# Attention scores and values of 24 float32 heads moved from half-array to full-array matrix products

## Chip, cores and metric

One NeuronCore of one Trainium2 chip runs the whole program. The metric is the device time of one execution in microseconds (us), given as the median of three runs. Its engines appear below under the names of the profile: PE is TensorE (matrix products), PEld its weight loads, DVE is VectorE, ACT is ScalarE, POOL is GpSimd, and SP is SyncE, whose queue issues the transfers.

## What is computed

Windowed attention with a few always visible "sink" keys, and behind it a feed-forward layer with a cosine gate. Sizes: 4 batches, 8 heads, 768 positions, head size 64, window 128, 4 sink positions, model width 512, inner width 2048.

```python
scores = scale * np.matmul(q, k.transpose(0, 1, 3, 2))
keep = is_sink | in_window            # is_sink: key < 4; in_window: 0 <= query - key < 128
scores = np.where(keep, scores, -1000000000.0)
a = np.exp(scores - np.max(scores, axis=-1, keepdims=True))
a = a / (np.sum(a, axis=-1, keepdims=True) + 1e-09)
attn = np.matmul(a, v)                # heads are then laid side by side: x is 3072 x 512
h = x @ w_in
out = (h * np.cos(h)) @ w_out
```

## The kernel before

The 3072 rows are cut into 12 chunks of 256 queries (CB = 2 blocks of 128, NT = 256). A chunk has 8 heads, in 4 pairs, and then 8 "slots" of the dense layer: a slot computes 256 of the 2048 inner columns (h, 24 products of 256 columns, L381), gates them on ACT and DVE, and adds them to the two output accumulators (acc, 12 products of 512 columns, L429). Precision is kept by splitting operands in a rounded high part and a remainder (xhi and xlo, whi and wlo, ghi and glo), each in the one-pass type float32r, and three products for one.

The first 24 heads (NEH = 24: the first chunk of batches 0, 1 and 2) are done otherwise, in plain float32: `o.early`. For a pair of them:

- q and k of both heads are loaded in natural layout, turned on PE (qk, L713), and copied to tq and tk: rows 0 to 63 hold the even head's features, rows 64 to 127 the odd one's.
- Scores (`scores_pe`, L737): for each head and each of its 2 query blocks j one product with 64 rows of contraction, 128 keys wide for j = 0 and 256 for j = 1, into the one PSUM buffer "s". DVE adds the mask and takes the row minimum (L806), ACT takes the exponential, then the rows are scaled and turned on PE (tp, L895) and copied to pt.
- Values (`values_pe`, L925): two products for each head, one of 256 and one of 128 columns, with v32 as the stationary operand of 64 columns, into the even or odd half of a PSUM tile x.f of 64 partitions (tag "av", one buffer).
- Split (`split_x`): ACT rounds the head to xhi (L319), PE subtracts it in place by a product with minus the identity (`x_minus`, L327: 64 x 64 for the even head, 128 x 64 for the odd one), and ACT or DVE copies what remains to xlo.

In the trace a plain float32 product shows as two instructions, so 48 score products of each width are 96 score instructions, and 48 value products are 96.

Weights arrive as 64-bit numbers in 32 pieces of 512 KB ("raw", two buffers); DVE and ACT turn each into whi and wlo. They are needed slot by slot in the first dense chunk, so the first 150 us hold weight conversion, the early heads and the first dense slots together. 160 filler products (idle, L1172) stand in PE's program where the planner saw PE without work.

The order on every engine is set by a planner ahead of time (`Plan.order`): each step has engines with estimated durations, dependencies, buffers and a priority (its due time). Each engine then runs its list strictly in that order, and SP's list of transfers likewise. The constants in C (due times, penalties) are not touched by the change.

Of the kernel before, what the change touches and what calls it, by code (L numbers as in the profile page):

```python
# [16 lines left out]
P = 128  # L17
# [20 lines left out]
def f32(ap):  # L38
    return ap.bitcast(F32)
# [7 lines left out]
class Plan:  # L47
# [21 lines left out]
    def order(self, gate=0.0):  # L69
# [103 lines left out]
def attn_moe_kernel(ctx, tc, q, k, v, n_sink, window, w_in, w_out, out):  # L173
# [33 lines left out]
    xk_t = lp.tile([P, 4 * KB, 32], F32, name="xk")  # L207
    v32s = [lp.tile([P, KB, D], F32, name=f"v32_{n}") for n in range(C["XV"])]
    xb = lp.tile([64, NT], F32, name="xb")
# [112 lines left out]
    def x_minus(x, p, odd):  # L322
        def fn(e):


            r, c = slice(0, odd * 64 + 64), slice(odd * 64, odd * 64 + 64)
            nc.tensor.matmul(  # L327
                out=x.f[p][:, odd], lhsT=minus[r, c], rhs=x.hi[r, p, :], start=False, stop=True, skip_group_check=True
            )
        return fn  # L330

    def x_lo(x, a, p, odd):
        def fn(e):
            if p == 0 and not odd:
                x.lo = xp.tile([P, NP, NT], F32R, name=f"xlo_{a}", tag="xlo", bufs=2)
            if odd is None:
                e.tensor_tensor(out=x.lo[:, p, :], in0=x.f[p], in1=f32(x.hi)[:, p, :], op=ALU.subtract)
            else:
                copy(e, x.lo[odd * 64 : odd * 64 + 64, p, :], x.f[p][:, odd])
        return fn  # L340

    def split_x(plan, x, a, p, t, odd=None):

        add, buf = plan.add, plan.buf
        if p == 0 and not odd:
            x.bhi, x.blo = buf("xhi", 2), buf("xlo", 2)
        i = add(
            [("ACT", act(NT, odd is None))], x_hi(x, a, p, odd), x.sums[p] + (x.firsts[:1] if x.parts else [x.bhi]), t
        )
        users = [i]  # L350
        d = [i, x.firsts[1] if x.parts else x.blo]
        if odd is None:
            j = add(sub(NT), x_lo(x, a, p, odd), d, t + 0.3, port=True)
        else:
            m = add([("PE", 0.11)], x_minus(x, p, odd), [i], t + 0.3)
            users.append(m)
            env.minus.users.append(m)
            j = add([("ACT", act(NT, False)), ("DVE", dve(NT))], x_lo(x, a, p, odd), d + [m], t + 0.6)
        if not x.parts:
            x.firsts = [i, j]  # L360
        if odd:
            x.parts[p] += [i, j]
        else:
            x.parts.append([i, j])
        return users + [j]


# [234 lines left out]
    def banded_path():  # L602
# [80 lines left out]
        def load_v(o):  # L683
# [6 lines left out]
            return fn  # L690

        def q_turn(o):
            def fn(e):
# [37 lines left out]
        def scores_pe(o, oe, j):  # L731
# [55 lines left out]
        def scores(o, j):  # L787
            def fn(e):
                i, w = o.i0 + j, o.w[j]
                o.s_ps[j] = ps.tile([P, BW], F32, name=f"s_{o.tag}_{j}", tag="s")  # L790
                c0 = max(i - 1 - o.kb0, 0) * o.sw
# [175 lines left out]

        env.minus, bgt = buf("gt", 1), buf("gt", 1)
        bgt.users.append(add([("POOL", 0.4)], lambda e: e.memset(f32(gt), 0.0), [bgt], 0.0))
# [16 lines left out]
        def before_softmax(g, o):  # L986
# [15 lines left out]
            if o.early:  # L1002
                if o.odd == 0:
# [6 lines left out]
                    bb.users.append(q0)  # L1010
                    bx, o.btk = buf("xk", 1), buf("tk", 1)
                    src = lambda c: k[o.b, o.h + c, o.kb0 * P : (o.kb0 + o.nkb) * P, :]
# [5 lines left out]
                    bx.users.append(i)  # L1018
                    k0 = add(
                        [("ACT", act(o.nkb * P, False)), ("DVE", dve(o.nkb * P))], k_out(o), [i, o.btk],  # L1020
                        t - 6 * T + C["DQ"] + 1.6,
                    )
                    bb.users.append(k0)
                    o.kr = [q0, k0]
            else:
# [33 lines left out]
            for j in range(CB):  # L1059
                bs = buf("s", 1)  # L1060
                if o.early:
                    oe = heads[g - o.odd]
                    dur, fn, deps, used = o.w[j] / 600 + 0.02, scores_pe(o, oe, j), oe.kr, (oe.btq, oe.btk)
                else:
                    dur, fn, deps, used = 0.23, scores(o, j), [o.ql, *o.kr], (o.bl, b1, b2)
                c0 = add([("PE", dur)], fn, [*deps, bs], t - 5 * T + C["DS"] + (3.25, 5.55)[j])
                for bb in used:
                    bb.users.append(c0)
                c1 = add(
# [28 lines left out]
        def after_softmax(g, o):  # L1098
            x, t = xs[o.a], head_time(g)
            bx = buf("v32", C["XV"])  # L1100
            o.bxv = bx
            i = add(dma(1), load_v(o), [bx], t - 2 * T + C["DV"] + 3.2, lat=2.4)
            if o.early:
                pt, bpt = buf("tp", 1), buf("phi", 1)
                p0 = add([("PE", 0.107 * o.n)], turn(o), o.nm + [pt], t + C["DA"] + 1.3)
# [10 lines left out]
                x.y0 = y0  # L1116
                bx.users.append(y0)
                bpt.users.append(y0)
# [289 lines left out]
```

## Time and profile before

| what | value |
|---|---|
| runs | 781.53, 781.53 and 782.52 us; median 781.53 |
| profiled execution | span 781.0 us, first to last instruction; its own time is not listed apart from the runs, whose median lies 0.5 us above the span |
| PE busy | 761.2 us, 97% of the span |
| DVE, ACT, POOL busy | 601.6, 580.7 and 152.4 us (77%, 74%, 20%) |
| filler products (L1172) | 160, from 9.9 to 70.8 us |
| early heads' PE work (L737, L925, L327) | from 13.2 to 188.3 us |

A busy share says how long an engine had an instruction in work. PE's instructions overlap, so what a product costs is read from the start of one instruction to the start of the next in the timeline, not from its listed duration. In the timeline 128*64 means 128 rows of contraction and 64 stationary columns, and "128x256" behind it is the output.

### The profile page before, as it was taken

How to read it: one execution, taken by the hardware profiler on the slowest of the kernel's cores; microseconds unless marked ns; L12 is line 12 of the kernel's file. 1: busy time of each engine (PE TensorE's matmuls, PEld its weight loads, DVE VectorE, ACT ScalarE, POOL GpSimd, SP SyncE). 2: the span in 40 equal slices, each digit the busy share in tenths (PEclk: the TensorE clock that was granted, in tenths of full speed). 3: DMA queues.
4: the chain of work that ended last, by engine and by line, in shares of the span. 5: the costliest groups of instructions: out<-in, count | busy, mean ns of one | idle time of the engine just before them, and what ended most of it. 6: DMA issues, size and time to landing. Idle time of an engine off the chain costs nothing.

```text
span 781.0 us, 15456 instructions
## 1 busy us (share of the span) xinstructions
PE 761.2 (97%) x5087; PEld 674.4 (86%) x5087; DVE 601.6 (77%) x1587; ACT 580.7 (74%) x1344; POOL 152.4 (20%) x250
## 2 busy tenths in 40 slices
PE   7999999999999999999999999999999999999996
PEld 6766767788989888998999999999999999999994
DVE  5777788876868979879889988878879888865431
ACT  1667866688788787887886888888798888795332
POOL 1112300110223122223233222312212222200000
PEclk9999999999999999999999999999999999999998
DMA  5554455323254376357356452331243233110000
GB/s 150 151 159 136 143 148 171 86 59 69 43 148 116 76 159 159 75 137 182 78 127 171 95 117 46 57 78 33 42 86 54 43 78 60 27 36 6 28 1 32
DMA packets 215674, 71.51 MB, mean 92 GB/s; under 512 B 204320, under 2 KB 204320, under 8 KB 215584
## 3 DMA queue, kind: packets, MB, share of 16 engines
q1 hardware_dynamic: 215584, 70.43, 37.8%
q8 instruction: 42, 0.69, 0.4%
q14 instruction: 48, 0.39, 0.2%
HBM read 64.10 MB, written 6.29 MB: 90 GB/s over the span
## 4 chain that ended last, share of the span: by engine, by line
PE 87%; DMA 4%; ACT 3%; DVE 3%; issue 1%; SPq 1%; DVEq 0%; ACTq 0%
PE h L381 33%; PE acc L429 30%; PE av L949 5%; PE tp L895 5%; PE s L793 4%; PE idle L1172 3%; PE s L737 3%; DMA raw<-in_moe_w_in_dram 2%; PE av L925 2%; PE qk L713 1%; DMA xq<-in_q_dram 1%; PE gp L877 1%; DMA raw<-in_moe_w_out_dram 1%; SPq L662 1%; PE av L327 1%
## 5 line engine op out<-in xcount | busy, mean ns | idle before, releaser
L381 PE MATMUL h<-xhi,whi_in 128*128 128x256 f32 x768 | 225.0, 293 | 2.4 <-DVE glo L420 2.3
L381 PE MATMUL h<-xlo,whi_in 128*128 128x256 f32 x768 | 217.0, 283 | 0.0
L381 PE MATMUL h<-xhi,wlo_in 128*128 128x256 f32 x768 | 216.7, 282 | 0.0
L381 PEld LDWEIGHTS h<-xhi,whi_in 128*128 128x128 f32 x768 | 145.6, 190 | 15.6 <-DVE glo L420 4.0
L429 PE MATMUL acc<-whi_out,ghi 128*128 128x512 f32 x384 | 155.5, 405 | 0.0
L381 PEld LDWEIGHTS h<-xhi,wlo_in 128*128 128x128 f32 x768 | 146.0, 190 | 7.3
L429 PE MATMUL acc<-wlo_out,ghi 128*128 128x512 f32 x384 | 151.5, 395 | 0.0
L429 PE MATMUL acc<-whi_out,glo 128*128 128x512 f32 x384 | 150.2, 391 | 0.0
L381 PEld LDWEIGHTS h<-xlo,whi_in 128*128 128x128 f32 x768 | 145.6, 190 | 0.0
L806 DVE CUSTOM_DVE_ANT_0 p<-s,mk 128x264 f32<-128x264 f32 (+1 forms) x192 | 76.9, 401 | 33.9 <-PE s L793 20.8
L815 ACT ACTIVATE p<-p,st 128x264 f32<-128x264 f32 (+1 forms) x192 | 93.4, 490 | 0.6
L420 DVE TENSOR_TENSOR glo<-h,ghi 128x512 fp32r<-128x512 f32 x96 | 65.7, 684 | 34.8 <-ACT ghi L414 34.5
L429 PEld LDWEIGHTS acc<-whi_out,glo 128*128 128x128 f32 x384 | 72.1, 188 | 16.2
L403 ACT ACTIVATE r<-r,neg 128x512 f32<-128x512 f32 x96 | 69.1, 724 | 19.4 <-DVE r L396 19.0
L414 ACT CAST ghi<-h 128x512 fp32r<-128x512 f32 x96 | 55.8, 582 | 30.9 <-PE acc L429 29.4
L408 DVE TENSOR_TENSOR h<-h,r 128x512 f32<-128x512 f32 x96 | 66.2, 691 | 15.2 <-ACT r L403 14.6
L396 DVE SCALAR_TENSOR_TENSOR r<-h,yt 128x512 f32<-128x512 f32 x96 | 65.5, 683 | 15.3 <-ACT yt L390 14.6
L429 PEld LDWEIGHTS acc<-whi_out,ghi 128*128 128x128 f32 x384 | 72.5, 189 | 5.4 <-issue 0.3
L429 PEld LDWEIGHTS acc<-wlo_out,ghi 128*128 128x128 f32 x384 | 72.9, 190 | 4.0
L390 ACT ACTIVATE yt<-h 128x512 int32<-128x512 f32 x96 | 57.1, 595 | 22.2 <-PE h L381 21.5
L835 POOL TENSOR_SCALAR p<-p,st 128x264 f32<-128x264 f32 (+2 forms) x71 | 38.2, 553 | 148.9 <-DVE st L825 118.1
L848 POOL TENSOR_TENSOR vr<-v,vr 128x192 fp32r<-128x192 f32 (+1 forms) x61 | 36.2, 594 | 154.3 <-ACT vr L843 149.9
(127 smaller groups left out, 1417.7 us busy)
## 6 DMA issues: line engine op xcount, KB each, us to landing
raw<-in_moe_w_in_dram SPq DMA_DIRECT2D x32, 512.0 KB
raw<-in_moe_w_out_dram SPq DMA_DIRECT2D x32, 512.0 KB
xk<-in_k_dram SPq DMA_DIRECT2D x256, 48.0 KB
out_dram<-raw SPq DMA_DIRECT2D x24, 256.0 KB
v<-in_v_dram SPq DMA_DIRECT2D x64, 96.0 KB
xq<-in_q_dram SPq DMA_DIRECT2D x144, 32.0 KB
v<-in_v_dram SPq DMA_DIRECT2D x32, 64.0 KB
xq<-in_q_dram SPq DMA_DIRECT2D x24, 64.0 KB
```

Source lines behind the costliest of these rows:

```text
L381: nc.tensor.matmul(out=o.h[:, t, :], lhsT=w[:, c, fs], rhs=xx[:, c, :], start=(c == 0 and n == 0), stop=(c == NC - 1 and n == 2),)
L390: nc.scalar.activation(out=yt, in_=o.h, func=AF.Copy, scale=INV2PI, bias=0.25)
L396: nc.vector.scalar_tensor_tensor(out=o.r, in0=o.h, scalar=INV2PI, in1=yt, op0=ALU.mult, op1=ALU.subtract)
L403: nc.scalar.activation(out=o.r, in_=o.r, func=AF.Sin, scale=TWOPI_DOWN, bias=quarter)
L408: nc.vector.tensor_tensor(out=o.h, in0=o.h, in1=o.r, op=ALU.mult)
L414: nc.scalar.copy(out=o.ghi, in_=o.h)
L420: e.tensor_tensor(out=o.glo, in0=o.h, in1=f32(o.ghi), op=ALU.subtract)
L429: nc.tensor.matmul(out=x.acc[j], lhsT=gg[:, t, j * P : (j + 1) * P], rhs=w[:, f, :], start=(f == 0 and n == 0), stop=(f == NFT - 1 and n = ...
L806: nc.vector.tensor_tensor_reduce(out=o.p[:, j, :w], in0=o.s_ps[j][:, :w], in1=masks[min(o.i0 + j, 2)][:, :w], op0=ALU.add, op1=ALU.min, sc ...
L815: nc.scalar.activation(out=o.p[:, j, :w], in_=o.p[:, j, :w], func=AF.Exp, bias=o.lead.st[:, 0, o.nth, j : j + 1], scale=-1.0, accum_out=o. ...
L895: nc.tensor.transpose(out=o.tp[:, n * P : (n + 1) * P], in_=o.p[:, i - o.i0, c0 : c0 + P], identity=ident)
L949: nc.tensor.matmul(out=dst, lhsT=lhs, rhs=rhs, start=(n == 0), stop=(n == len(seq) - 1), skip_group_check=True)
```

## The change

Only the 24 float32 heads change.

- k is written to a tile kz of two halves, zero but for its own head: the even head's k in rows 0 to 63 of half 0, the odd one's in rows 64 to 127 of half 1 (two copies of 64 rows in place of one of 128). kz is cleared once by POOL. One product with 128 rows of contraction then gives both heads' scores of a query block, 2 x 128 or 2 x 256 columns wide. The PSUM buffer "s" becomes a whole bank with one half for each head.
- Both heads' v lie side by side as 128 stationary columns, loaded by one step of two transfers that takes both v buffers. Each head's value products now fill 128 partitions of x.f, of which the head's own 64 are used.
- The subtraction is one product for a pair, 128 x 128, with xhi repeated over both halves (512 columns). It waits for both heads' xhi, and both copies to xlo wait for it.
- The planner counts one step where there were two, and doesn't make a step that takes two buffers of a kind wait for itself.

```diff
-                behind[taker[b0]].append(taker[b1])
-                wait[taker[b1]] += 1
+                if taker[b0] != taker[b1]:
+                    behind[taker[b0]].append(taker[b1])
+                    wait[taker[b1]] += 1
...
-                nc.scalar.copy(out=x.hi[odd * 64 : odd * 64 + 64, p, :], in_=x.f[p][:, odd])
+                r = slice(odd * 64, odd * 64 + 64)
+                nc.scalar.copy(out=x.hi[r, p, :], in_=x.f[p][r, odd])
...
-            r, c = slice(0, odd * 64 + 64), slice(odd * 64, odd * 64 + 64)
             nc.tensor.matmul(
-                out=x.f[p][:, odd], lhsT=minus[r, c], rhs=x.hi[r, p, :], start=False, stop=True, skip_group_check=True
+                out=x.f[p], lhsT=minus, rhs=x.hi[:, p, :].unsqueeze(1).broadcast_to([P, 2, NT]),
+                start=False, stop=True, skip_group_check=True,
             )
...
-                copy(e, x.lo[odd * 64 : odd * 64 + 64, p, :], x.f[p][:, odd])
+                r = slice(odd * 64, odd * 64 + 64)
+                copy(e, x.lo[r, p, :], x.f[p][r, odd])
...
+        m = add([("PE", 0.232)], x_minus(x, p), [x.head, i], t + 0.3)
...
+        for half in range(2):
+            d = [m] + x.firsts[1:2] if x.firsts[1:] else [m, x.blo]
+            j = add([("ACT", act(NT, False)), ("DVE", dve(NT))], x_lo(x, a, p, half), d, t + 0.6 + 0.01 * half)
...
+        def load_v_pair(o, o1):
+            def fn(e):
+                dst = v32_t.rearrange("p a n d -> p (a n d)")[:, : o.nkb * 2 * D]
+                o.v2 = o1.v2 = dst.rearrange("p (n c) -> p n c", c=2 * D)
+                for h in range(2):
+                    nc.sync.dma_start(
+                        out=dst.rearrange("p (n h d) -> p n h d", n=o.nkb, d=D)[:, :, h, :],
+                        in_=v[o.b, o.h + h, o.kb0 * P : (o.kb0 + o.nkb) * P, :].rearrange("(n s) d -> s n d", s=P),
+                    )
...
-        def k_out(o):
-            def fn(e):
-                o.tk = ap.tile([P, o.nkb, o.sw], F32, name=f"tk_{o.tag}", tag="tk")
-                copy(e, o.tk.rearrange("p n s -> p (n s)"), o.qk[:, 1, : o.nkb * P])
+        def k_out(o, odd):
+            def fn(e):
+                r = slice(odd * 64, odd * 64 + 64)
+                copy(e, env.kz[r, odd, : o.nkb * P], o.qk[r, 1, : o.nkb * P])
...
-                o.s_ps[j] = ps.tile([P, BW], F32, name=f"s_{o.tag}_{j}", tag="s")
-                c0 = max(i - 1 - o.kb0, 0) * o.sw
-                r = slice(o.odd * 64, o.odd * 64 + 64)
+                s_ps = ps.tile([P, 2, NT], F32, name=f"s_{o.tag}_{j}", tag="s")
+                o.s_ps[j], o1.s_ps[j] = s_ps[:, 0], s_ps[:, 1]
+                c0 = max(i - 1 - o.kb0, 0) * P
                 nc.tensor.matmul(
-                    out=o.s_ps[j][:, :w], lhsT=oe.tq[r, j * P : (j + 1) * P],
-                    rhs=oe.tk.rearrange("p n s -> p (n s)")[r, c0 : c0 + w], start=True, stop=True,
+                    out=s_ps[:, :, :w], lhsT=o.tq[:, j * P : (j + 1) * P], rhs=env.kz[:, :, c0 : c0 + w],
+                    start=True, stop=True,
                 )
...
-                    x.f[o.pair] = ps.tile([64, 2, NT], F32, name=f"av_{o.tag}", tag="av")
+                    x.f[o.pair] = ps.tile([P, 2, NT], F32, name=f"av_{o.tag}", tag="av")
...
-                    mms.append((dst, o.v32[:, kb - o.kb0, :], o.pt[:, o.offs[n] * P : o.offs[n + 1] * P]))
+                    mms.append((dst, o.v2[:, kb - o.kb0], o.pt[:, o.offs[n] * P : o.offs[n + 1] * P]))
...
+                o.bxs = [buf("v32", C["XV"]) for _ in range(C["XV"])]
+                o.vl = add(dma(2), load_v_pair(o, heads[g + 1]), o.bxs, t - 2 * T + C["DV"] + 3.2, lat=2.4)
...
+        env.kz = ap.tile([P, 2, NT], F32, name="kz", tag="plo")
+        nc.gpsimd.memset(env.kz, 0.0)
```

The planner writes the order anew. First place, PE at the beginning of the program: the scores of the first pair, heads 0 and 1 of batch 0. In a name, s_0_1_0 is batch 0, head 1, query block 0; the last number is a buffer. Before:

```order
L737 MATMUL s_0_0_0_221<-tk_0_0_211,tq_0_0_198 128x128
L1172 MATMUL idle<-gt 128x256 x10
L737 MATMUL s_0_0_1_242<-tk_0_0_211,tq_0_0_198 128x256
L1172 MATMUL idle<-gt 128x256 x7
L713 MATMUL qk_0_2_253<-ident,xq 128x128 x2
L1172 MATMUL idle<-gt 128x256
L737 MATMUL s_0_1_0_261<-tk_0_0_211,tq_0_0_198 128x128
L1172 MATMUL idle<-gt 128x256 x4
L713 MATMUL qk_0_2_253<-ident,xk 128x128 x2
L1172 MATMUL idle<-gt 128x256 x4
L737 MATMUL s_0_1_1_279<-tk_0_0_211,tq_0_0_198 128x256
```

Now:

```order
L1208 MATMUL idle<-gt 128x256 x12
L760 MATMUL s_0_0_0_229<-kz,tq_0_0_199 128x2x128
L1208 MATMUL idle<-gt 128x256 x14
L736 MATMUL qk_0_2_255<-ident,xq 128x128 x2
L760 MATMUL s_0_0_1_258<-kz,tq_0_0_199 128x512
L736 MATMUL qk_0_2_255<-ident,xk 128x128 x2
L1208 MATMUL idle<-gt 128x256 x12
L760 MATMUL s_0_2_0_290<-kz,tq_0_2_268 128x2x128
```

Four products for the pair have become two, twice as wide, under the name of the even head; the second stands between the turns of the next pair's q and k, where the third stood.

Second place, PE at the first pair's values: av is its PSUM tile, tp are turned probabilities, the rows with gt are the subtraction. Before:

```order
L925 MATMUL av_0_0_412<-pt_0_0_383,v_0_76 64x256
L925 MATMUL av_0_0_412<-pt_0_0_383,v_0_76 64x128
L1172 MATMUL idle<-gt 128x256 x4
L737 MATMUL s_0_5_0_425<-tk_0_4_374,tq_0_4_368 128x128
L1172 MATMUL idle<-gt 128x256 x2
L925 MATMUL av_0_0_412<-pt_0_1_420,v_1_77 64x256
L925 MATMUL av_0_0_412<-pt_0_1_420,v_1_77 64x128
L327 MATMUL av_0_0_412<-xhi_427,gt 64x256
L1172 MATMUL idle<-gt 128x256
L737 MATMUL s_0_5_1_443<-tk_0_4_374,tq_0_4_368 128x256
L1172 MATMUL idle<-gt 128x256
L327 MATMUL av_0_0_412<-xhi_427,gt 64x256
```

Now, from the odd head's last value product to the next pair's first one:

```order
L948 MATMUL av_0_0_412<-pt_0_1_423,v_76 128x128
L1208 MATMUL idle<-gt 128x256 x4
L918 MATMUL tp_0_2_450<-ident,p_0_2_299 128x128 x3
L736 MATMUL qk_0_0_456<-ident,xq 128x128 x2
L760 MATMUL s_0_6_0_459<-kz,tq_0_6_431 128x2x128
L736 MATMUL qk_0_0_456<-ident,xk 128x128 x2
L329 MATMUL av_0_0_412<-xhi_425,gt 128x512
L918 MATMUL tp_0_3_472<-ident,p_0_3_315 128x128 x3
L1208 MATMUL idle<-gt 128x256 x3
L760 MATMUL s_0_6_1_487<-kz,tq_0_6_431 128x512
L1208 MATMUL idle<-gt 128x256 x4
L948 MATMUL av_0_2_502<-pt_0_2_461,v_76 128x256
```

The outputs of the values went from 64 to 128 partitions. The two subtractions, between which score products of a later pair stood, became one of 512 columns behind both heads' values, and four more rows stand between it and the next pair's values.

Third place, SP's list of transfers around the v loads of the second and third pair (raw: weight pieces, v: the early heads' v). Before:

```order
L705 DMA xq<-in_q_dram 128x2x64 x2
L705 DMA xk<-in_k_dram 128x2x64 x2
L686 DMA v_0_76<-in_v_dram 128x2x64
L474 DMA raw_70<-in_moe_w_in_dram 128x1024
L686 DMA v_1_77<-in_v_dram 128x2x64
L474 DMA raw_71<-in_moe_w_in_dram 128x1024
L705 DMA xq<-in_q_dram 128x2x64 x2
L705 DMA xk<-in_k_dram 128x2x64 x2
L474 DMA raw_70<-in_moe_w_in_dram 128x1024
L686 DMA v_0_76<-in_v_dram 128x2x64
L474 DMA raw_71<-in_moe_w_in_dram 128x1024
L686 DMA v_1_77<-in_v_dram 128x2x64
```

Now:

```order
L728 DMA xq<-in_q_dram 128x2x64 x2
L728 DMA xk<-in_k_dram 128x2x64 x2
L486 DMA raw_70<-in_moe_w_in_dram 128x1024
L709 DMA v_76<-in_v_dram 128x2x64 x2
L728 DMA xq<-in_q_dram 128x2x64 x2
L728 DMA xk<-in_k_dram 128x2x64 x2
L486 DMA raw_71<-in_moe_w_in_dram 128x1024
L486 DMA raw_70<-in_moe_w_in_dram 128x1024
L728 DMA xq<-in_q_dram 128x2x64 x2
L709 DMA v_76<-in_v_dram 128x2x64 x2
```

A pair's two v transfers, which stood apart with a weight piece between them, are issued together, once for a pair.

## Rows read from the trace of the kernel before

**Rows 1.** The page: busy time by engine, and the chain that ended last.
```profile
PE 761.2 (97%) x5087; PEld 674.4 (86%) x5087; DVE 601.6 (77%) x1587; ACT 580.7 (74%) x1344; POOL 152.4 (20%) x250
...
PE 87%; DMA 4%; ACT 3%; DVE 3%; issue 1%; SPq 1%; DVEq 0%; ACTq 0%
```

**Rows 2.** Busy time of each engine (us, instructions) in four stretches.
```profile
core 0: us, PE busy (x) PEld busy (x) DVE busy (x) ACT busy (x) POOL busy (x), PEclk, DMA share, GB/s
10.00:190.00 180.00, 175.85 (x1026) 136.98 (x1025) 140.91 (x355) 124.12 (x307) 24.74 (x32) 0.99 0.47 128
190.00:700.00 510.00, 506.40 (x3578) 466.42 (x3578) 426.55 (x1162) 425.42 (x984) 123.36 (x203) 1.00 0.40 90
116.90:120.10 3.20, 3.20 (x16) 2.98 (x15) 2.73 (x9) 3.08 (x12) 0.51 (x1) 0.50 1.00 236
...
100.00:150.00 50.00, 47.13 (x261) 36.28 (x261) 42.75 (x95) 31.73 (x71) 3.00 (x3) 0.97 0.49 146
```

**Rows 3.** Groups by shape, 10 to 200 us: busy us, mean ns | idle before.
```profile
L1172 PE MATMUL idle<-gt 128*128 128x256 f32 x160 | 29.6, 313 | 0.0
...
L737 PEld LDWEIGHTS s<-tk,tq 64*128 64x128 f32 x96 | 14.5, 189 | 9.0 <-issue 2.5 <-DVE st L806 2.1 <-DVE wt L482 0.5
L925 PEld LDWEIGHTS av<-pt,v 128*64 128x64 f32 x96 | 11.2, 136 | 10.7 <-issue 2.2 <-ACT pt L370 1.4 <-ACT xhi L319 1.1
...
L319 ACT CAST xhi<-av 64x256 fp32r<-64x256 f32 x24 | 8.7, 364 | 7.4 <-PE av L925 3.4 <-PE av L327 2.7 <-PE s L737 1.0
...
L370 ACT COPY tk<-qk 128x256 f32<-128x256 f32 x11 | 4.2, 378 | 1.2 <-PE qk L713 1.1
```

**Rows 4.** Timeline of TensorE, 63.5 to 87 us: start, us, what.
```profile
63.82 0.28 PE L381 MATMUL h<-xlo,whi_in 128*128 128x256 f32 x1
64.03 0.48 PE L737 MATMUL s<-tk,tq 64*128 64x128 f32 x2
...
64.67 0.28 PE L381 MATMUL h<-xhi,wlo_in 128*128 128x256 f32 x1
64.79 0.27 PE L381 MATMUL h<-xlo,whi_in 128*128 128x256 f32 x1
...
65.25 0.38 PE L713 MATMUL qk<-ident,xq 128*128 128x128 f32 x2
...
65.59 0.28 PE L381 MATMUL h<-xhi,wlo_in 128*128 128x256 f32 x1
...
79.35 0.33 PE L327 MATMUL av<-xhi,gt 64*64 64x256 f32 x1
...
79.94 0.39 PE L429 MATMUL acc<-wlo_out,ghi 128*128 128x512 f32 x1
80.17 0.40 PE L429 MATMUL acc<-whi_out,glo 128*128 128x512 f32 x1
...
82.03 0.86 PE L925 MATMUL av<-pt,v 128*64 128x256 f32 x4
...
83.05 0.28 PE L381 MATMUL h<-xhi,wlo_in 128*128 128x256 f32 x1
...
85.67 0.28 PE L327 MATMUL av<-xhi,gt 128*64 128x256 f32 x1
85.88 0.70 PE L737 MATMUL s<-tk,tq 64*128 64x256 f32 x2
...
86.73 0.28 PE L381 MATMUL h<-xhi,wlo_in 128*128 128x256 f32 x1
```

**Rows 5.** Timeline of TensorE around 45 us, two products that start together.
```profile
44.84 0.48 PE L737 MATMUL s<-tk,tq 64*128 64x256 f32 x1
44.85 0.33 PE L327 MATMUL av<-xhi,gt 64*64 64x256 f32 x1
```

**Rows 6.** Timeline of TensorE around 115 us, a wait.
```profile
115.30 0.70 PE L737 MATMUL s<-tk,tq 64*128 64x256 f32 x2 [1.31 <-DVE st L806]
```

**Rows 7.** The chain in order of time: a load behind two weight pieces.
```profile
3.07 6.39 DMA xq<-in_q_dram
```

More of the change, by code (lines that the diff above doesn't have):

```diff
@@ L207, in attn_moe_kernel @@
     xk_t = lp.tile([P, 4 * KB, 32], F32, name="xk")
-    v32s = [lp.tile([P, KB, D], F32, name=f"v32_{n}") for n in range(C["XV"])]
+    v32_t = lp.tile([P, C["XV"], KB, D], F32, name="v32")
+    v32s = [v32_t[:, n] for n in range(C["XV"])]
     xb = lp.tile([64, NT], F32, name="xb")
@@ L318, in fn, with x_minus @@
             else:
-                nc.scalar.copy(out=x.hi[odd * 64 : odd * 64 + 64, p, :], in_=x.f[p][:, odd])
+                r = slice(odd * 64, odd * 64 + 64)
+                nc.scalar.copy(out=x.hi[r, p, :], in_=x.f[p][r, odd])
         return fn
-    def x_minus(x, p, odd):
+    def x_minus(x, p):
         def fn(e):
-            r, c = slice(0, odd * 64 + 64), slice(odd * 64, odd * 64 + 64)
             nc.tensor.matmul(
-                out=x.f[p][:, odd], lhsT=minus[r, c], rhs=x.hi[r, p, :], start=False, stop=True, skip_group_check=True
+                out=x.f[p], lhsT=minus, rhs=x.hi[:, p, :].unsqueeze(1).broadcast_to([P, 2, NT]),
+                start=False, stop=True, skip_group_check=True,
             )
@@ L349, in split_x @@
         )
+        if odd == 0:
+            x.head, x.first_hi = i, x.parts == []
+            if x.first_hi:
+                x.firsts, x.parts = [i], [[]]
+            else:
+                x.parts.append([])
+            return [i]
         users = [i]
-        d = [i, x.firsts[1] if x.parts else x.blo]
         if odd is None:
[L353 to L363, printed above, removed]
-            x.parts.append([i, j])
-        return users + [j]
+            j = add(sub(NT), x_lo(x, a, p, odd), [i, x.firsts[1] if x.parts else x.blo], t + 0.3, port=True)
+            if not x.parts:
+                x.firsts = [i, j]
+            x.parts.append([i, j])
+            return users + [j]
+        m = add([("PE", 0.232)], x_minus(x, p), [x.head, i], t + 0.3)
+        users.append(m)
+        env.minus.users.append(m)
+        for half in range(2):
+            d = [m] + x.firsts[1:2] if x.firsts[1:] else [m, x.blo]
+            j = add([("ACT", act(NT, False)), ("DVE", dve(NT))], x_lo(x, a, p, half), d, t + 0.6 + 0.01 * half)
+            if not x.firsts[1:]:
+                x.firsts.append(j)
+            users.append(j)
+        x.parts[p] += [x.head] + users
+        return users
     def copy(e, dst, src):
@@ L1018, in before_softmax @@
                     bx.users.append(i)
[L1019 to L1024, printed above, removed]
+                    kk = []
+                    for half in range(2):
+                        kk.append(add(
+                            [("ACT", act(o.nkb * P, False)), ("DVE", dve(o.nkb * P))], k_out(o, half),
+                            [i] + (kk or ([o.bkz] if g else [o.bkz, bkz])), t - 6 * T + C["DQ"] + 1.6 + 0.01 * half,
+                        ))
+                    bb.users += kk
+                    o.kr = [q0, *kk]
             else:
@@ L1059, in before_softmax @@
             for j in range(CB):
[L1060 to L1063, printed above, removed]
-                else:
[L1065 to L1068, printed above, removed]
+                if o.early and o.odd:
+                    oe = heads[g - 1]
+                    c0, bs = oe.sc[j]
+                else:
+                    bs = buf("s", 1)
+                    if o.early:
+                        o1 = heads[g + 1]
+                        dur, fn, deps, used = 4 * 2 * o.w[j] / 2400, scores_pe(o, o1, j), o.kr, (o.btq, o.bkz)
+                    else:
+                        dur, fn, deps, used = 0.23, scores(o, j), [o.ql, *o.kr], (o.bl, b1, b2)
+                    c0 = add([("PE", dur)], fn, [*deps, bs], t - 5 * T + C["DS"] + (3.25, 5.55)[j])
+                    o.sc = getattr(o, "sc", []) + [(c0, bs)]
+                    for bb in (*used, bkz) if o.early else used:
+                        bb.users.append(c0)
                 c1 = add(
@@ L1099, in after_softmax @@
             x, t = xs[o.a], head_time(g)
-            bx = buf("v32", C["XV"])
-            o.bxv = bx
-            i = add(dma(1), load_v(o), [bx], t - 2 * T + C["DV"] + 3.2, lat=2.4)
+            if o.early and o.odd == 0:
+                o.bxs = [buf("v32", C["XV"]) for _ in range(C["XV"])]
+                o.vl = add(dma(2), load_v_pair(o, heads[g + 1]), o.bxs, t - 2 * T + C["DV"] + 3.2, lat=2.4)
+            elif not o.early:
+                bx = buf("v32", C["XV"])
+                o.bxv = bx
+                i = add(dma(1), load_v(o), [bx], t - 2 * T + C["DV"] + 3.2, lat=2.4)
             if o.early:
+                i, bxs = (o if o.odd == 0 else heads[g - 1]).vl, (o if o.odd == 0 else heads[g - 1]).bxs
                 pt, bpt = buf("tp", 1), buf("phi", 1)
@@ L1116, in after_softmax @@
                 x.y0 = y0
-                bx.users.append(y0)
+                for bx in bxs:
+                    bx.users.append(y0)
                 bpt.users.append(y0)
```

9 lines of the change are left out of this document (5 added, 4 removed).

## The prediction

> **What bounds the kernel now.** I read the page first: PE has work in 761.2 of 781 us, and the chain that ended last lies on PE for 87% [rows 1]. So what PE is spared is spared to the kernel, wherever PE does not then wait. Then I read the stretches. The early float32 heads lie in the first 190 us. From 10 to 190 us PE shows 175.85 us of work in 180, but DVE with 140.91 and ACT with 124.12 are not far behind; after it, where the change touches nothing but the order, PE works 506.40 of 510 us [rows 2]. What the change saves can therefore only be saved before 190 us, and the later stretch hands it on unchanged to the end. Last I read PE's timeline, start to start, for what one product costs [rows 4]. There the reader sees that a steady dense product of 256 columns takes 0.12 us (64.67 to 64.79), one of 512 columns 0.23 us (79.94 to 80.17), and that products on part of the array cost far more than their columns.
>
> **What each early product costs now** [rows 4]. Each sum runs from the product before to the second product behind, since both neighbours are held up too.
> - Scores, 128 keys: 63.82 to 64.67 is 0.85 us and holds two dense products besides; 0.85 - 0.24 = 0.61 us.
> - Scores, 256 keys: 85.67 to 86.73 is 1.06 us, with a small product before and a dense one behind; 1.06 - 0.24 = 0.82 us.
> - A head's values, four instructions: 82.03 to 83.05 is 1.02, less one dense product 0.90. The change-over ahead is that of the scores (63.82 to 64.03 is 0.21 in place of 0.12), so 0.99 us.
> - The even head's subtraction on 64 x 64: 79.35 to 79.94, less 0.23, and 0.09 ahead, is 0.45 us. The odd head's on 128 rows costs no more than its columns, 0.12 us.
>
> **What they cost on the full array.** No float32 product on 128 x 128 stands in the trace outside the start, so this is bounded by the nearest row, the turns of q: two full-array float32 instructions of 128 columns and one dense product take 65.25 to 65.59, hence 0.11 us for each turn [rows 4]. The columns are the same as before, so a pair's scores are 2 instructions of 256 columns (0.44 us together) and 2 of 512 (0.88), a head's values 768 columns (0.66), the one subtraction 0.23. Against before:
> - scores of a pair: 2 x (0.61 + 0.82) - 1.32 = 1.54, 12 pairs: 18.5 us
> - values: 0.99 - 0.66 = 0.33, 24 heads: 7.9 us
> - subtraction: 0.45 + 0.12 - 0.23 = 0.34, 12 pairs: 4.1 us
>
> The sum is 30.5 us of PE's time. It counts each change-over as if it stood alone, and some do not: one even subtraction begins 0.01 us behind a score instruction [rows 5]. I take nine tenths, **27 us**, with 20 and 30.5 as the bounds.
>
> The Trainium skill (TensorEngine Tiling (Array Packing), Key Properties) says that parts of the array work independently and can run products in parallel, which speaks against filling the array with zeros. The trace shows such a pair of products [rows 5], and its cost is what the cut to nine tenths stands for.
>
> **What it adds.** k is copied in two pieces of 64 rows, 0.364 us each by the nearest row, where one of 128 rows took 0.378 [rows 3]; 12 x 0.35 = 4.2 us, nearly all on ACT. ACT has 56 us to spare before 190 us, so I count 0; without that cover it would be 4.2. The clearing of kz goes to POOL, busy 24.74 of 180 us [rows 2]: 0, at worst a microsecond once. The masks, exponentials and copies to xlo are as many as before. The single "s" buffer is now held for two masks, but only twice in a pair instead of four times: 0.
>
> Two waits are new, and both end at the next pair's first value product. The even head's xlo can't be copied before the odd head's values are done, so the av buffer comes free one copy later, 0.36 us. And a pair's v can be asked for only when the last pair's values are done. The new order leaves PE about 4.0 us of work in between (second place of the change, from its second row: 11 fillers at 0.12, 10 turns at 0.11, a subtraction of 0.23, scores of 0.44 and 0.88 us). I take 0.1 us for each of the 11 gaps between pairs, 1 us in all, between 0 and the rival below.
>
> **How much of 27 us arrives.** If PE lost no time to new waits, 10 to 190 us would shrink to 153 us, and DVE would have to do its 140.91 us in that, 92%. The trace shows what DVE carries while PE stays full: 426.55 of 510 us, 84%, in the later stretch. It also shows a stretch where it did not: from 100 to 150 us DVE is at 42.75 of 50, 86%, and PE lacks 2.9 us [rows 2], of which 1.31 is a score product that waited for DVE to free its buffer [rows 6]. Just behind, the granted clock stands at 0.50 for 3.2 us [rows 2], the lower of the two levels, 1.2 in place of 2.4 GHz, which loses half of that. So I let DVE fill up to 86%: 140.91 / 0.86 = 164 us, **16 us** less than 180. Less 1 us for the new waits, **15 us**. The 160 fillers, 29.6 us of PE's busy time [rows 3], are in PE's list in both versions and cancel out.
>
> Against the profiled span: 781.0 - 15 = 766.0 us; the median of the runs lies 0.5 us above the span, so **766.5 us**.
>
> **The rivals.**
> - *All of it arrives.* DVE and ACT wait for PE now (the mask sits behind the scores), and shorter products end these waits; then the whole 27 us comes through: 754.5 us. For it: 39 of DVE's 180 us are not work. Against it: the 100 to 150 us stretch. Chance 0.15.
> - *The other engines take most of it.* If DVE can't be filled above 80% while weights, masks and dense steps wait for each other, 140.91 / 0.80 = 176 us, a gain of 4 us: 777.5 us. For it: 78% is all it reaches over the 180 us now. Against it: 84% later. Chance 0.20.
> - *Bare weight loads.* Value products load 128 columns in place of 64: 189 against 136 ns [rows 3]. If these loads don't hide, 96 x 0.053 = 5.1 us of the 27 go, and the scores' second instruction keeps some of its hold-up; the lower bound of 20 gives 15 x 20 / 27 = 11 us, 770.5 us. Against it: the turns load 128 columns every 0.11 us. It lies inside the first range below, and I give it no chance apart. The Trainium skill (TensorE: Matmul & The Clock Gate, LDWEIGHTS) says that a load's time goes by its columns and not by its rows. By that the loads double, an estimate of 5 us from its figure; the two load rows agree in direction, though not with a factor of two.
> - *Slower: the v loads.* With no second buffer the two transfers start when a pair's values end. A small load behind two weight pieces took 6.39 us [rows 7], so one behind a single piece may take half, 3.2 us, and one behind two misses the 4.0 us by 2.4. The price is 11 gaps times the miss; from a mean miss of 1.4 us it eats the 15 us. At 2 us it is 22 us, and the kernel takes 788 us. Against it: no wait of PE for v stands in the chain now, and a weight piece isn't always under way. Chance 0.08.
> - *No change.* That the products don't become what the diff says is excluded by the new order, which shows them 512 columns wide. What is left is that the waits of PE that follow from a faster PE bring the lower clock again and again, 1.6 us each time [rows 2]: nine of them would cancel 15 us. Chance 0.05.
>
> **How the numbers follow.** The forecast (a gain of 10 to 20 us, 761.5 to 771.5) has 0.52, all 0.15, most taken 0.20, no change 0.05, slower 0.08. 0.2% is 1.6 us, about what a measurement of this kernel tells from no change. Faster: 0.52 + 0.15 + 0.20 = 0.87; same 0.05; slower 0.08. The range leaves out the slower case and a little of the others: 755 to 779 us. The gaining cases alone reach from 751 to 779.
>
> **What would show it right or wrong.** A score product of a pair should take 0.44 and 0.88 us start to start with no hold-up of its neighbours; a head's values 0.66; the subtraction 0.23. If they do and the first dense products still end at the same time, the step on DVE's share is wrong, and DVE's and ACT's waits say for what. The place to look at is PE's waiting ahead of the first value product of each pair: over 1 us there, ended by a v load or by xlo, is the slower rival. From 190 us on the slots should follow each other as before; a difference there would be one of the new order that I didn't foresee. The gain should have its full size at 190 us and keep it.

## The result

The changed kernel takes 770.75 us (769.23 to 773.15, 4 runs) where the kernel before took 782.02 us (781.53 to 783.73, 4 runs): a ratio of 0.9856, 95% interval 0.9835 to 0.9877. That is 11.3 us of gain; 766.5 us were forecast, with 755 to 779 as the range. The profiled execution took 770.14 us, its span 768.7 us. The four times go with the mean granted clock of their execution: 769.23 us at 0.990, 773.15 us at 0.985.

### The profile page after: what moved, and what is told of

Read it like the earlier page. It is cut to its first block, busy times and chain, and to the rows that moved or that the text cites. A ratio compares the mean times of both kernels' runs of the same rounds, so it can differ in the third digit from the quotient of the medians.

```text
span 768.7 us, 15296 instructions
## 1 busy us (share of the span) xinstructions
PE 740.4 (96%) x5027; PEld 669.1 (87%) x5027; DVE 610.1 (79%) x1606; ACT 579.1 (75%) x1350; POOL 140.4 (18%) x234
## 4 chain that ended last, share of the span: by engine, by line
PE 79%; DVE 7%; ACT 6%; DMA 5%; issue 2%; SPq 1%; DVEq 0%
PE h L393 30%; PE acc L441 29%; PE av L972 5%; PE tp L918 4%; PE s L816 4%; DMA xk<-in_k_dram 2%; PE av L948 2%; PE idle L1208 1%; ACT p L838 1%; PE s L760 1%; DMA v<-in_v_dram 1%; DVE p L829 1%; DMA xq<-in_q_dram 1%; PE gp L900 1%; DVE glo L432 1%
## 5 line engine op out<-in xcount | busy, mean ns | idle before, releaser
L408 DVE SCALAR_TENSOR_TENSOR r<-h,yt 128x512 f32<-128x512 f32 x96 | 65.4, 682 | 14.4 <-ACT yt L402 13.8
L871 POOL TENSOR_TENSOR vr<-v,vr 128x192 fp32r<-128x192 f32 (+1 forms) x57 | 33.8, 592 | 159.6 <-ACT vr L866 145.1
L816 PE MATMUL s<-r,l 128*128 128x264 f32 (+2 forms) x288 | 61.0, 292 | 0.2
```

The costliest lines, as they stand in the source:

```text
L408: nc.vector.scalar_tensor_tensor(out=o.r, in0=o.h, scalar=INV2PI, in1=yt, op0=ALU.mult, op1=ALU.subtract)
L816: nc.tensor.matmul(out=o.s_ps[j][:, :w], lhsT=o.l[:, j * P : (j + 1) * P], rhs=r.rearrange("p n s -> p (n s)")[:, c0 : c0 + w], start=(n = ...
```

## The profile of the changed kernel

The page, the rows that answer to [rows 1]: the first is PE's busy time, the second and third the chain that ended last, by engine and by line.

```profile
PE 740.4 (96%) x5027; PEld 669.1 (87%) x5027; DVE 610.1 (79%) x1606; ACT 579.1 (75%) x1350; POOL 140.4 (18%) x234
PE 79%; DVE 7%; ACT 6%; DMA 5%; issue 2%; SPq 1%; DVEq 0%
PE h L393 30%; PE acc L441 29%; PE av L972 5%; PE tp L918 4%; PE s L816 4%; DMA xk<-in_k_dram 2%; PE av L948 2%; PE idle L1208 1%; ACT p L838 1%; PE s L760 1%; DMA v<-in_v_dram 1%; DVE p L829 1%; DMA xq<-in_q_dram 1%; PE gp L900 1%; DVE glo
```

PE lies on 79% of the chain, no longer 87%, and loads of k and v stand in it now. The stretches, to be held against [rows 2] (busy time and count for each engine, then the granted clock):

```profile
10.00:190.00 180.00, 168.44 (x1058) 146.03 (x1057) 149.27 (x390) 141.20 (x340) 21.10 (x26) 0.98 0.48 130
190.00:700.00 510.00, 507.62 (x3587) 465.59 (x3586) 435.61 (x1165) 415.73 (x976) 116.11 (x195) 1.00 0.39 89
```

From 190 to 700 us PE is as full as it was. In the first stretch it now lacks 11.6 us of 180, where it lacked 4.1. PE's timeline shows what the new products cost (start, duration, and the idle time ahead in brackets if there is any):

```profile
42.53 0.28 PE L393 MATMUL h<-xlo,whi_in 128*128 128x256 f32 x1
42.65 1.02 PE L760 MATMUL s<-kz,tq 128*128 128x512 f32 x2
43.11 0.68 PE L393 MATMUL h<-xhi,whi_in 128*128 128x256 f32 x1
43.63 0.28 PE L393 MATMUL h<-xhi,wlo_in 128*128 128x256 f32 x1
...
60.00 0.60 PE L760 MATMUL s<-kz,tq 128*128 128x256 f32 x2
60.25 0.47 PE L393 MATMUL h<-xhi,whi_in 128*128 128x256 f32 x1
60.55 0.28 PE L393 MATMUL h<-xhi,wlo_in 128*128 128x256 f32 x1
...
61.86 0.82 PE L948 MATMUL av<-pt,v 128*128 128x256 f32 x4
62.43 0.36 PE L393 MATMUL h<-xhi,whi_in 128*128 128x256 f32 x1
62.63 0.28 PE L393 MATMUL h<-xhi,wlo_in 128*128 128x256 f32 x1
```

Read as in the prediction, from an early product's start to that of the second product behind it, less the 0.12 us of the dense product in between: a pair's scores of 256 keys take 0.98 - 0.12 = 0.86 us, those of 128 keys 0.55 - 0.12 = 0.43, a head's values 0.77 - 0.12 = 0.65. The start of the product ahead is not held up (42.53 to 42.65). The subtraction takes 0.23 us where nothing disturbs it (from 174.22 to 174.45). Forecast were 0.88, 0.44, 0.66 and 0.23.

To see how far this arrives I take the same points of the work in both traces. PE's last dense product for the 16th copy of gated values to ghi starts at 195.75 us before and at 179.76 after, 16.0 us earlier; the copy itself starts at 202.63 before and at 188.01 after, 14.6 earlier, as ACT and DVE take 8.25 us from that product to the copy in place of 6.88. PE's last product starts at 773.19 before and at 759.60 after, 13.6 earlier; the span is 12.3 us shorter.

The largest wait of PE, in PE's timeline:

```profile
101.84 0.58 PE L329 MATMUL av<-xhi,gt 128*128 128x512 f32 x1
104.02 0.38 PE L393 MATMUL h<-xhi,whi_in 128*128 128x256 f32 x1 [1.61 <-DVE glo L432]
...
106.88 0.28 PE L393 MATMUL h<-xlo,whi_in 128*128 128x256 f32 x1
110.33 1.09 PE L918 MATMUL tp<-ident,p 128*128 128x128 f32 x3 [3.17 <-ACT p L856]
111.07 0.78 PE L441 MATMUL acc<-whi_out,ghi 128*128 128x512 f32 x1
```

and what DVE did at that time:

```profile
106.91 0.58 DVE L789 STREAM_TRANSPOSE tk<-xk 128x384 f32<-128x384 f32 x1 [0.81 <-DMA xk<-in_k_dram]
107.41 0.65 DVE L506 SCALAR_TENSOR_TENSOR wt<-raw,wt 128x512 int32<-128x512 int32 x1
107.98 0.68 DVE L530 TENSOR_TENSOR wlo_out<-wt,whi_out 128x512 fp32r<-128x512 f32 x1
108.58 1.02 DVE L847 TENSOR_SCALAR st<-st 128x8 f32<-128x8 f32 x1
109.64 0.20 DVE L848 RECIPROCAL st<-st 128x8 f32<-128x8 f32 x1
```

PE's turns of p wait for ACT to normalize p, ACT for the reciprocals on DVE, and these stand in DVE's list behind three other steps, of which the first waited 0.81 us for a load of a late head's k. DVE runs its list in order, so the steps behind the waiting one waited with it. Just behind this wait, from 110.0 to 113.4 us, the granted clock was 0.5, and products of 512 columns start 0.43 us apart where they start 0.23 apart else.

PE's waits from 13 to 190 us, by what ended them (total us, times, longest):

```profile
PE tp L918 <- ACT p L856: 3.2, 1, 3.2
PE av L948 <- DMA v<-in_v_dram: 1.9, 2, 1.2
PE h L393 <- DVE glo L432: 1.8, 2, 1.6
PE qk L736 <- DMA xk<-in_k_dram: 1.4, 1, 1.4
PE av L948 <- ACT pt L382: 1.4, 2, 0.8
```

No single one is large. v cost 1.9 us in two waits, not eleven.

**The ledger.** For each run of early products in either trace I took the time from the dense product ahead to the second one behind, less the dense products' own 0.12 or 0.23 us and less the gaps, and left the late heads' products out. Before the change these runs take 60 us in all, after it 39, so 21 us of PE's time are gone from the trace. At the undisturbed costs above they would take 12 x (0.43 + 0.86 + 0.23) + 24 x 0.65 = 34 us, so 60 - 34 = 26 us were to be spared; 27 were forecast. Of the 26, some 5 went into hold-ups around the early products that show no gap (39 - 34), since the rows' modelled ends overlap the next start by some 0.16 us, and 7.5 into gaps of PE (4.1 before, 11.6 after, from 13 us on). Nine dense products of 0.23 us, 2.1 us, stand behind the last product for the 16th copy in the new order and stood ahead of it in the old one. 26 - 5 - 7.5 + 2.1 = 15.6, near the 16.0 us by which that product comes earlier.

## The experiments

All were timed beside the kernel before; the ratios are to that kernel, and the changed kernel's own is 0.9856. A difference of 0.003, or 2.3 us, between two ratios is about what they can tell.

**The array's form undone in the changed order.** Theory A: the full array spares the time. Theory B: the pairing, with its new order, does.

```diff
+ for h in range(2):   # scores: two products, both on rows 0 to 63
+     out=s_ps[:, h, :w], lhsT=o.tq[0:64, ...], rhs=env.kz[0:64, h, ...]
+ r = slice(o.odd * 64, o.odd * 64 + 64)   # values: 64 columns
+     dst = x.f[o.pair][r, o.odd, ...], o.v2[:, kb - o.kb0, r]   # and start=(n == 0), for each head
+ for h in range(2):   # subtraction: 64 x 64, then 128 x 128
+     out=x.f[p][r, h], lhsT=minus[r, r], rhs=x.hi[r, p, :]
```

> The changed kernel with its order, buffers and waits, but the products back on part of the array: a pair's scores as two products with 64 rows (both read the even head's rows, so the odd head's scores come out as zeros), values with 64 stationary columns, the subtraction as 64 x 64 and 128 x 128 with 256 columns each. Theory A (the gain is the array's shape: a product on part of the array holds up its neighbours): the PE time saved goes again, and the time returns to 780 to 784 us. Theory B (the gain comes from pairing, that is from fewer steps and the planner's new order, and the shape is free): 770 to 773 us as the changed kernel.

Measured: 782.73 us, ratio 0.9994 (0.9976 to 1.0011). The whole gain is gone, and theory B falls as far as the time goes. PE's timeline of this kernel shows a second thing:

```profile
44.34 0.28 PE L394 MATMUL h<-xlo,whi_in 128*128 128x256 f32 x1
44.55 1.13 PE L763 MATMUL s<-kz,tq 64*128 64x256 f32 x4
45.61 0.38 PE L394 MATMUL h<-xhi,whi_in 128*128 128x256 f32 x1
45.83 0.28 PE L394 MATMUL h<-xhi,wlo_in 128*128 128x256 f32 x1
```

Both heads' scores in a row take 45.83 - 44.34 - 2 x 0.12 = 1.25 us, where two heads apart took 2 x 0.82 [rows 4]: the change-over is paid once for two. By the ledger's sum the early products take 54 us here, so pairing alone spared PE 6 us, and next to none of them shows in the median time. (In the profiled execution, 779.98 us and one of the two fastest of twelve, the last copy to ghi does start 4.4 us earlier than before the change.) The full array spared another 15 by the traces, 20 at undisturbed costs, and brought 11.

**One part undone each.** The same edits one at a time.

> Only the scores back to 64 rows (both products read the even head's rows, so the odd head's scores come out as zeros). Theory A: scores are 18.5 of the 30.5 us of PE time that the sum gave, so 0.6 of the 11.3 us go: 777.5 us, between 775 and 780. Theory B: no change, 770 to 773.

Measured: 777.33 us, ratio 0.993 (0.9906 to 0.9955).

> Only the values back to 64 stationary columns. Theory A: 7.9 of 30.5 us, a quarter of the gain: 773.7 us, between 772 and 776. Theory B: no change.

Measured: 778.49 us, ratio 0.9934 (0.9912 to 0.9957): a loss, as theory A says, but outside its range of 772 to 776. The product itself costs what the prediction had for it:

```profile
63.62 0.28 PE L393 MATMUL h<-xlo,whi_in 128*128 128x256 f32 x1
63.83 0.86 PE L949 MATMUL av<-pt,v 128*64 128x256 f32 x4
64.62 0.39 PE L393 MATMUL h<-xhi,whi_in 128*128 128x256 f32 x1
64.84 0.28 PE L393 MATMUL h<-xhi,wlo_in 128*128 128x256 f32 x1
```

64.84 - 63.62 - 2 x 0.12 = 0.98 us for a head.

> Only the subtraction back to one product of 64 x 64 and one of 128 x 128, both behind the odd head as in the changed kernel. Theory A: 4.1 of 30.5 us: 772.3 us, between 771 and 774. Theory B: no change.

Measured: 772.48 us, ratio 0.9863 (0.9843 to 0.9883). Against 0.9856 this gives 5.8, 6.1 and 0.5 us, 12.4 together, near the 10.8 of all three at once. Scores and values matter alike, and the costs say why: in these orders a pair's scores stand in a row, which costs 0.83 and 1.25 us where the full array takes 0.43 and 0.86, so 12 pairs lose 9.5 us and not the 18.5 of theory A; 24 heads' values lose 24 x (0.98 - 0.65) = 7.9 us. The share of 18.5 was wrong for this edit, and that 777.33 met 777.5 is luck. The subtraction's share can't be told from nothing.

**Is it VectorE's load that keeps the rest?** The prediction said that DVE can be filled to 86% only. The last step of the weights' conversion was cut to 64 of 512 columns, in both kernels.

```diff
- out=t, in0=raw[:, :, 0], scalar=29, in1=t,
+ out=t[:, :64], in0=raw[:, :64, 0], scalar=29, in1=t[:, :64],
```

> The changed kernel, with the last step of the weights' conversion (low) done by VectorE on 64 of 512 columns: the weights' low bits are left out, every other instruction and the order stay. Some 0.57 us less of VectorE's time for each of about 32 pieces, 18 us in the first 150 us. If VectorE takes what TensorE saves before 190 us (my theory of why 27 us of TensorE's time gave 11): 5 to 10 us faster than the changed kernel, about 761 to 766 us. Rival, TensorE is still the bound there and saved less than I worked out: 0 to 2 us, 769 to 771 us. Rival, waits for single transfers (v, x) took it: 0 to 3 us, and these waits stay in the timeline.

> The same cut of VectorE's work in the kernel before. It is the control: there TensorE had only 4 us of gaps before 196 us, so by the theory that VectorE binds only after the change it gains 0 to 3 us, 780 to 783 us. Were it to gain as much as the changed kernel does by the same cut, VectorE's work would cost alike in both, and would not explain where the saving went.

Measured: the changed kernel 768.81 us, ratio 0.982 (0.980 to 0.984); the kernel before 783.05 us, 1.001 (0.9995 to 1.0025). From 10 to 190 us:

```profile
10.00:190.00 180.00, 170.08 (x1055) 147.23 (x1054) 134.30 (x386) 140.14 (x339) 20.39 (x26) 0.97 0.49 130
```

DVE does 15 us less (134.30 for 149.27), the kernel gains 2 to 3, hardly more than two ratios can tell. The control gains nothing, so a little of DVE's work may count since the change, but it isn't what sets the pace. Where the 2 to 3 us arise is not seen: in the profiled execution the last copy to ghi starts at 754.22 us, in the changed kernel at 754.13, though the clock also stood at 0.50 from 69.6 to 73.0 us here and not there. The theory of VectorE's share falls.

**Is it TensorE itself?** One filling product in place of 160. The planner then writes other lists, too: the changed kernel's differ on every engine from some 30 us to the end, those of the kernel before on PE up to 190 us.

```diff
- "FILL": 160
+ "FILL": 1
```

> The changed kernel with 1 filling product in place of 160 (they compute nothing; 18 to 19 us of TensorE's time come off its list before 190 us). If TensorE is no longer the bound there: 0 to 4 us faster, 767 to 771 us, with the fillers' time turned into waits; slower, if TensorE's clock falls in those waits. Rival, TensorE still sets the pace: 10 us or more, 760 us or less.

> The kernel before with 1 filling product in place of 160. There TensorE sets the pace before 190 us, so the fillers' 18 to 19 us should count for more than in the changed kernel: 6 to 15 us faster, 768 to 776 us. If it gains no more than the changed kernel does, the other engines' pace is the same bound in both, and the full-array products saved the time in another way than by TensorE's busy time.

Measured: the changed kernel 780.40 us, ratio 0.9962 (0.9941 to 0.9982); the kernel before 787.29 us, 1.0064 (1.0045 to 1.0082). Both became slower, 8 us and 5 us, though 18 us left PE's list. From 10 to 80 us, the changed kernel so edited:

```profile
10.00:80.00 70.00, 51.78 (x220) 35.67 (x219) 57.61 (x165) 47.15 (x133) 12.08 (x12) 0.93 0.56 158
```

and the kernel before so edited:

```profile
10.00:80.00 70.00, 62.03 (x214) 38.06 (x213) 48.98 (x144) 37.57 (x111) 8.37 (x10) 0.59 0.51 143
```

In the first, PE has work for only 51.78 of 70 us: up to its last product for the 16th copy its gaps grew from 11.6 to 21.9 us, so a good part of the fillers' time turned into waits. In the second the clock stood at the lower level, 1.2 GHz, from 8.9 to 53.3 and from 60.1 to 73.8 us (0.59 on average; 1.00 in the same stretch with the fillers), and the same products took longer; PE had work for 4.69 of the 8.93 us ahead of the first fall and for 4.96 of the 6.83 us between the two stretches. Both expectations of a gain were wrong. Whether PE's own list still sets the pace in the first 80 us stays open all the same. For the kernel before, the clock hides the answer. For the changed kernel, the new order does: of the 9.2 us by which the last copy to ghi comes later than in the changed kernel, only 4.3 are there at the 16th copy, and the rest arises behind it, where no filler stood.

**Is it the loads, or both other engines' load?** Three edits of the changed kernel.

```diff
  # after_freeall: turns and values read a constant
- in_=tile...[:, m * 2 * D : (m + 1) * 2 * D]
+ in_=ident
- mms.append((dst, o.v2[:, kb - o.kb0], ...
+ mms.append((dst, ident, ...
  # after_lean, with the cut of DVE's step above
- func=AF.Sin
+ func=AF.Exp if o.m < 16 else AF.Sin
  # after_v2c: two places for a pair's v
- o.bxs = [buf("v32", C["XV"]) for _ in range(C["XV"])]
+ o.bxs = [buf("v2", 2)]
- i = add(dma(4), load_k(o), [bx], ...
+ i = add(dma(4), load_k(o), [bx, *early_y[-4:]], ...
```

> The changed kernel, in which the early heads' turns and value products read the identity matrix in place of the loaded q, k and v; the loads stay, but no early product waits for one any more and none waits for a product to free its place. The attention of the early heads is left out of the result in this way. If the single places for v, q and k cost what the waits in the trace show (1.44, 1.22 and 0.73 us, 3.4 together, and the chain of waits that lies on loads of k and v four times): 3 to 5 us faster, 766 to 768 us. If the chain only names loads whose end falls together with other work: 0 to 1 us, 770 to 771 us.

Measured: 770.34 us, ratio 0.9845 (0.9828 to 0.9862): nothing that can be told. PE's waits from 13 to 190 us in it:

```profile
PE s L760 <- DVE st L829: 3.6, 4, 1.4
PE av L948 <- ACT pt L382: 2.4, 2, 1.9
PE tp L918 <- ACT p L856: 2.4, 1, 2.4
PE h L393 <- DVE glo L432: 1.8, 2, 1.6
```

The waits for the early heads' loads are gone, and those for the masks, 0.4 us in the changed kernel, are 3.6 now. Two kinds of load stay: those of the late heads, one of which stood at the head of the 3.17 us wait above, and the weights'.

> The changed kernel with less work for VectorE and ScalarE in the first stretch: the weights' low bits as in the earlier cut (15 us of VectorE), and the first 16 sines computed as exponentials, so that ScalarE loads no function table before 190 us (15 loads of 1.28 us, 19 us of its 141). The order stays. VectorE alone gave 2 us. If ScalarE is what the shorter products wait for (tp on the normalized p 3.17 us, values on pt 1.4 us, h on glo 1.61 us stand in the trace): 5 to 8 us faster than the changed kernel, 763 to 766 us. If neither engine's load is the cause: as the earlier cut alone, 768 to 769 us.

Measured: 769.42 us, ratio 0.9834 (0.9816 to 0.9852), no better than the cut on DVE alone.

```profile
10.00:190.00 180.00, 169.98 (x1071) 147.80 (x1070) 136.64 (x394) 121.11 (x325) 20.20 (x26) 0.98 0.49 130
```

ACT does 20 us less, DVE 13 us less, and the stretch is hardly shorter.

> The changed kernel with two places for a pair's v (in room that the early heads leave unused), so that its load no longer waits for the last pair's value products. Only waits of value products for v can go: 1.95 us in the trace, two of them. 1 to 3 us faster than the changed kernel by the theory that these waits hold the following work up, 768 to 770 us; 0 if other waits take their place.

Measured: 786.74 us, ratio 1.0056 (1.0039 to 1.0072), 16 us slower. The edit moved more than the wait: late k loads had to follow the early values, since they share the room that I took for v, and the planner set a new order. PE's waits from 190 to 260 us:

```profile
PE s L821 <- DVE l L788: 3.6, 1, 3.6
PE tp L923 <- POOL p L863: 3.4, 1, 3.4
```

In the changed kernel PE waits 1.7 us in that stretch. The 16th copy came at 183.3 us here, 4.7 us earlier than in the changed kernel; but PE had run 2 products of the late heads' scores ahead of it where the changed kernel has run 22, so part of this lead was borrowed from later work. The loss came later, where the late heads begin, and the run says nothing on v itself.

**No early product waits for its input.** The last and widest cut.

```diff
- lhsT=o.tq[:, j * P : (j + 1) * P], rhs=env.kz[:, :, c0 : c0 + w]
+ lhsT=ident, rhs=ident.unsqueeze(1).unsqueeze(1).broadcast_to([P, 2, w // P, P])
  # likewise v, pt, and the inputs of all early turns
```

> The changed kernel, in which every early product of TensorE but the subtraction (turns of q, k and p, scores, values) reads the identity matrix in place of its inputs. The loads, copies, masks and exponentials stay, and so do each engine's order and the number and width of the products; the attention of the early heads is left out of the result. TensorE then waits in the first 190 us only for places in its banks and for the dense steps. If waits for the inputs of the early products are what gives the saving back (8 of the 11.6 us of gaps in the trace, and shorter ones that no row shows): 6 to 12 us faster than the changed kernel, 759 to 765 us. Rival, the places in the banks and the dense steps wait for the same masks, copies and gates, and take the waits over: 0 to 3 us, 768 to 771 us.

Measured: 771.91 us, ratio 0.9856 (0.9832 to 0.9881): the rival. PE's waits from 13 to 190 us in it:

```profile
PE h L393 <- DVE glo L432: 2.0, 2, 1.6
PE s L760 <- DVE st L830: 1.8, 4, 0.9
PE av L952 <- ACT xhi L322: 1.7, 2, 1.5
PE acc L441 <- POOL wlo_out L530: 1.3, 1, 1.3
PE av L329 <- ACT xhi L322: 1.2, 3, 0.8
PE acc L441 <- ACT whi_out L527: 1.2, 1, 1.2
```

Places in the banks (masks, xhi) and the dense steps (gates, weights) have taken the waits over. Where PE stood 3.17 us for p in the changed kernel, it goes on here, and stands 1.16, 1.35 and 0.89 us for weights and a mask between 104 and 110 us. The 16th copy comes 1.8 us earlier than in the changed kernel, the last one 1.1 us later.

## Why the prediction came out as it did

- **What bounds the kernel, and where the gain can lie:** right. From 190 us on PE is as full as before, and the lead of the first stretch is handed on: 14.6 us at the 16th copy, 13.6 at PE's last product, 12.3 in the spans and 11.3 in the medians. A little is lost on the way, against "keep it". About 1 us of that is the choice of executions: the forecast took the time to lie 0.5 us above the span, but in every later run of the kernel before it lies 1.75 to 1.85 us above it, so the execution profiled there took some 782.8 us, more than the median.
- **What a product costs on part of the array and on all of it:** right to 0.02 us for each kind, and so was the cut to nine tenths: 26 us at undisturbed costs for 27 (21 by the traces as they are). My sum gave all of it to the full array, though; 6 of the 26 belong to heads that now stand side by side.
- **k copies and clearing at nothing:** ACT does 17 us more in 10 to 190 us, the copies of kz 8.4 of them in place of tk's 4.2, the rest being work that has moved forward (up to the 16th copy it is 141.1 us for 137.5). That it was covered is in keeping with the cut of ACT's work that brought nothing.
- **New waits, 1 us in all:** this is the term that failed. v's share was right in kind and small, 1.9 us. But PE's gaps grew by 7.5 us (nine waits of over 0.3 us, ended by seven different steps), and hold-ups that show no gap took some 5 more. Outside the first value product of a pair the prediction had only DVE's share to stand for waits.
- **DVE fills to 86%:** the step that failed in its reason. Its result, 11 us that don't arrive, stands beside 12.5 by the ledger; yet DVE reached 149.27 of 180 us, 83%, and with 15 us taken off it PE still lacked 10 us. I took a wait on DVE for a limit of DVE's capacity, and that the size came near is luck.
- **The rivals:** "all of it arrives" is refuted. "Other engines take most of it" named too small a gain, 4 us against 11.3, and its reason, DVE's share, falls with the cut of DVE's work. "Bare weight loads" named 770.5 us, and the likeness is chance: a head's values cost 0.65 us start to start although they load 128 columns four times, so the loads are hidden. The rule of the Trainium skill that a load's time goes by its columns (TensorE: Matmul & The Clock Gate, LDWEIGHTS) changed nothing here for that reason. "Slower by v" was wrong in price: two waits of 1.2 us at most. The low clock came once in mid-run for 3.4 us, as it had before. (From 7.6 to 14.4 us the granted clock of the changed kernel is 0.5 as well, and that of the kernel before is not; but the fillers from 9.9 to 11.1 us start 0.24 us apart in both traces, so the two kernels ran alike there.)

So the mechanism was right, the amount spared was right, and what arrives was sized 15 us for 11.3. What gives back the rest is narrowed down, not settled. It is not VectorE's load alone (2 to 3 us), not that of VectorE and ScalarE together, not the loads of the early heads, and not the inputs of the early products. These cuts left the order of all lists as it was, and those of the loads and the inputs uncovered other waits a little further on. I read this as the order: it lets several chains through PE, ACT and DVE end close together, and taking one away leaves the next. That is argued from what the cuts did not bring. The two runs in which the planner wrote other lists, without fillers and with v in two places, show only that other orders can cost 10 and 16 us.

One thing about the order can be read from the kernels. It was not left over from the old products. The planner wrote it anew, with a new duration for a step of scores (w is 128 or 256 keys):

```diff
-                    dur, fn, deps, used = o.w[j] / 600 + 0.02, scores_pe(o, oe, j), oe.kr, (oe.btq, oe.btk)
+                        dur, fn, deps, used = 4 * 2 * o.w[j] / 2400, scores_pe(o, o1, j), o.kr, (o.btq, o.bkz)
```

That is 0.23 and 0.45 us for one head before, where the trace shows 0.61 and 0.82, and 0.43 and 0.85 us for a pair now, where the trace shows 0.43 and 0.86. So the old lists were written as if the early products already cost little: 36 us in all for the 60 that they took, against 35 for 39 now. The planner saw no saving. In its own schedule, the starts that `Plan.order` works out from its durations, the 16th copy starts at 166.8 us before and at 168.3 us after; in the traces it starts 35.8 us later than that before, and 19.7 us later after. By the sums above, 24 us of this delay were the early products' (60 - 36), and 4 are now (39 - 35), 20 less; what is left of it grew from some 11 to some 15 us. These 4 us, with the 1.5 by which the planned copy itself moved back, are what the first stretch gives back of the 20. Why the remaining delay grew is not shown.

## What to carry to other kernels

A product on part of the array is to be priced with its neighbours, from the product ahead to the second behind. With zeros in the other half, and as many columns, a head's scores cost 0.22 and 0.43 us here in place of 0.61 and 0.82, and its values 0.65 in place of 0.99. If a planner orders the work, it needs that price too. What the bound engine is spared arrives only as far as the other queues are ahead of it; here 26 us became 11. When a lead shrinks so, one engine's busy share is a poor guide to how much is lost: take work off that engine first and see.

## What the runs showed of the hardware

- Products of 64 rows beside each other share their change-over: 1.25 us for two heads' 256 keys in a row, 1.64 us for the same apart.
- The same product cost the same in both orders: a head's values with 64 stationary columns took 0.99 us in the kernel before and 0.98 in the changed order, with 128 columns 0.65.
- Work that computes nothing can hold the clock. Without the fillers the kernel before ran at a mean granted clock of 0.59 from 10 to 80 us in place of 1.00, and was 5 us slower although PE had 18 us less to do; a part of its lists was in another order, too.
